# A block-diagonal inverse, a column-grouped projection and a segmented order in a gated mix of long convolution and local attention

## The chip, the cores and the metric

The kernel runs on one core of a Trainium2 chip. The metric is the time of one execution on the device, in microseconds. Three executions of the kernel before the change took 247.66, 249.07 and 249.46 us, so the median is 249.07. The profile comes from one more execution, which took 247.85 us; its instructions span 246.1 us.

Names used below: PE is the tensor engine (PEld its weight loads), DVE the vector engine, ACT the scalar engine, POOL the GpSimd engine, SP the engine that issues most of the DMAs.

## What is computed

With S = 2048 tokens, D = 640 channels and bf16 inputs:

```python
x = A_q
g = sigmoid((x * gate_w).sum(-1, keepdims=True))
# a: long convolution
k_shift = causal 4-tap filter of A_k with A_shift_k (per channel)
kv = k_shift * A_v
y  = irfft(rfft(pad(kv)) * rfft(pad(A_ssm_k)))[:S] + kv * A_ssm_D
a  = A_q * y
# b: 32 heads of 20, each token sees 8 keys at distance 0, 2, ..., 14
q, k, v = split(x @ B_wqkv)
b = softmax(local_scores(q, k) * 20**-0.5) @ v @ B_wo
out = g * a + (1 - g) * b
```

## The kernel before, in words

The long convolution is done as a transform of length 4096 in factors 32 x 64 x 2, with matmuls on PE. Channels are laid out as four groups of 160 on the four blocks of 32 partitions, with 32 positions of the first factor in each block. The channels are treated in two halves, P = 0 and P = 1.

- `xpose`, `vproj`, `qkproj` (L575) transpose x and project it. `fragger` (L614) moves pieces of projected q and k by DMAs from POOL into sets of four heads. `score_gen` (L636) makes scores, ACT takes their exponentials (L643), `pv_gen` (L664) multiplies them by v, and DVE normalises (L676: a product with the f32 reciprocal, repeated over the 20 channels of a head).
- `gate` (L542) computes the gate's logits with 20 matmuls of 128 rows by 32 columns, 512 wide, in the four column groups of PE; four DMAs on SP spread the result over `g_nat`, and DVE makes g and 1 - g of it.
- `conv` and `conv_v` make kv on DVE (L481, L488, L492).
- `h_stream` and `u_stream` transform the filter and kv: `s1_unit` (L697), then `s2_unit` (L713), each with a cast out of PSUM by ACT or DVE (L284, L286). `swaps` (L805, L807) exchange halves of the filter's spectrum between partitions through SP's DMA queue. `products` (L751) multiplies spectra on DVE.
- `inverse1` (L820) does the first half of the inverse transform, 10 units of 16 matmuls for each P, and casts the result into the tile UC.
- `op_tr` (L838) transposes the attention output into the tile oT; `outproj` (L854) projects it by wo in 16 tiles of 128 tokens: ten matmuls each, 512 and 128 columns wide, for five blocks of 128 channels. Each is scaled by 1 - g (`omg`) on its way to the tile bl (L858 on ACT, L860 on DVE). Tiles 4 to 15 come first, then 0 to 3.
- `load_q` (L873) loads q a second time, into the tile SX behind the filter's spectrum: token tiles 4 to 15 when the second transform stages are done, and 0 to 3 after the inverse's first half of P = 0, because they lie on what it reads.
- `final` does the rest for six groups of up to three token tiles. First the second half of the inverse (L893): for every token tile 32 matmuls of 32 rows by 32 columns, 160 wide, 512 in all, into two PSUM slots a group. Then six ACT activations of 128x320 with the scale g (L901), a product with q on DVE (L906), the sum with bl (L908), and four DMAs on SP (L911).

The order is not written out by hand. Every stage is a generator that yields requests (`Req`): the engines that may do it, an estimated cost, the events it depends on, and PSUM slots taken and given back (there are four, `Plan(4)`). `Plan.run` repeatedly picks the request with the smallest `start + 120 ns * priority` and emits its instructions. The instructions of each engine then run in that order, with semaphores for the real dependences. The priorities are one number for each stage (`PRI`); for casts that ACT or DVE may do, `lean` is added to ACT's estimated end. `paced` loads wait until the modelled DMA pipe is within `BG` ns of running dry. A request without work is given to "G" (POOL) or "S" (SP) at a cost of 1 ns.

The numbers of the planner are estimates of its author and are not measurements of this run. Its model of PE counts instructions (`mm`, a matmul and its weight load are two) and allows one page of `PAGE = 256` every `FETCH = 3600` ns.

Of the kernel before, what the change touches and what calls it, by code (L numbers as in the profile page):

```python
# [10 lines left out]
BF = mybir.dt.bfloat16  # L11
# [37 lines left out]
BG = 1266.0  # L49
# [6 lines left out]
def fft_consts():  # L56
# [24 lines left out]
    T = np.tile(T.reshape(32, 64 * 2 * 32), (4, 1))  # L81
# [49 lines left out]
class Req:  # L131


    def __init__(self, engs, cost=0.0, deps=(), take=0, give=(), n=0, move=0.0, pri=None, mode=None, bg=None, mm=0, lean=0.0):
        self.engs, self.cost, self.deps, self.take, self.give, self.n, self.move = engs, cost, deps, take, give, n, move
        self.pri, self.mode, self.bg, self.mm, self.lean = pri, mode, bg, mm, lean
# [4 lines left out]
LEAN_QK = -248.0  # L141
LEAN_V = 87.0
LEAN_H = -137.0
PRI = dict(loads=0, fragger=0, xpose=-9.2, score_gen=-8.6, pv_gen=-5.7, conv=-1.6, conv_v=-24.1, bulk=0, conv_end=0, qkproj=-4.2, vproj=-4.8,
           gate=-0.8, load_G=0, h_slot=0, p2_slot=10.2, u_slot=0, swaps=0, load_T=0, op_tr=4.7, outproj=37.5, load_q=0, products=6.3, final=-18.6,
           h_stream=(-3.7, -4.9), u_stream=(0.9, 2.5), inverse1=(33.7, 30.7))
# [4 lines left out]
class Plan:  # L151


    def __init__(self, nslots):
        self.at = dict(P=0.0, A=0.0, D=0.0, G=0.0, S=0.0, Q=0.0)
# [6 lines left out]
        self.lane = {"S": lane, "Q": lane, "G": []}  # L162
# [4 lines left out]
    def add(self, gen, pri):  # L167
        self.streams.append([pri, gen, next(gen)])
# [6 lines left out]
    def start(self, r, e):  # L175
# [3 lines left out]
        for d in r.deps:  # L179
            if d.t is None:  # L180
                return INF
            t = max(t, d.t + LAT.get((d.eng, e), 60.0))
# [9 lines left out]
    def best(self, r):  # L192
        found = []
        for e in r.engs:
            s = self.start(r, e)
            found.append((s + self.cost(r, e) + (r.lean if e == "A" else 0.0), s, e))
        end, s, e = min(found)
        return s + self.cost(r, e) if s < INF else INF, s, e

    def run(self):  # L200
        while self.streams:
            pick = None
            for k, (pri, gen, r) in enumerate(self.streams):
                end, st, e = self.best(r)
                if st == INF:
                    continue
                p = pri if r.pri is None else r.pri
# [5 lines left out]
            pri, gen, r = self.streams[k]  # L213
# [16 lines left out]
            self.at[e] = end  # L230
# [19 lines left out]
            try:  # L250
                self.streams[k][2] = gen.send(g)
            except StopIteration:
                del self.streams[k]
# [3 lines left out]
def kernel(  # L257
# [45 lines left out]
    g_nat = p0.tile([128, 16], F32, name="g_nat")  # L303
    omg = p0.tile([128, 16], F32, name="omg")
# [62 lines left out]
    def loads():  # L367
# [9 lines left out]
        for c in (1, 0):  # L377
            for q in range(4):
                yield from load(f"k{q}{c}", kin[32 * q:32 * q + 32, 3 + 32 * c:35 + 32 * c, :],
                                raw(k2, 32 * c * D + QC * q, [[64 * D, 32], [D, 32], [1, QC]]), 2000.0)  # L380
        for c in range(2):
            for q in range(4):
                yield from paced(f"v{q}{c}", vin[32 * q:32 * q + 32, c], raw(v2, QC * q + 80 * c, [[64 * D, 32], [D, 64], [1, 80]]), 2100.0)
        yield Req("S", 1.0, [ev("xtr")])
        h_lin = p0.tile([128, 80, 2, 64], BF, name="h_lin", tag="HL")
        st["h_lin"] = h_lin
        for P in range(2):
            for q in range(4):
                for c in range(2):
                    yield from paced(f"h{P}{q}{c}", h_lin[32 * q:32 * q + 32, PL * P:PL * P + PL, c, :],  # L390
                                     raw(A_ssm_k, (160 * q + 80 * c + PL * P) * S, [[64, 32], [S, PL], [1, 64]]), 1200.0)
# [12 lines left out]
    def load_G():  # L404
        yield Req("S", 1.0, [ev("conv"), ev("grow"), ev("vproj")])
# [9 lines left out]
    def load_T():  # L415
        yield Req("S", 1.0, [ev("p2")])
# [3 lines left out]
        yield Req("S", 1.0, [ev("hw1")])  # L420
        T = st["p2"].tile([128, 64, 2, 32], BF, name="T")
        st["T"] = T
        yield from load("T", st["T"][:], cf["T"].ap().rearrange("p (a r b) -> p a r b", a=64, r=2), 2700.0)
# [6 lines left out]
    def heads():  # L430
# [14 lines left out]
        for q in range(4):  # L445
            nc.gpsimd.dma_start(Dz[32 * q:32 * q + 1, :], raw(A_ssm_D, 160 * q, [[0, 1], [1, 160]]))
        for e in range(2):
            masks(e)
            if e == 0:
                for q in range(4):  # L450
                    nc.gpsimd.memset(kin[32 * q:32 * q + 1, 0:3, :], 0.0)
                    nc.gpsimd.dma_start(wraw[32 * q:32 * q + 32].rearrange("p c j -> p (c j)"), raw(A_shift_k, 4 * QC * q, [[0, 32], [1, 4 * QC]]))
# [499 lines left out]
```

## Time and profile before

| | us |
|---|---|
| three executions | 247.66, 249.07, 249.46 |
| profiled execution, on the device | 247.85 |
| its span of instructions | 246.1 |
| PE busy | 215.8 (88%) |
| DVE busy | 185.8 (76%) |
| ACT busy | 168.6 (69%) |
| POOL busy | 68.8 (28%) |
| PE in the chain that ended last | 49% of the span |
| mean granted PE clock | 0.9 |

The mean durations of a group overlap when instructions are pipelined; start-to-start distances in the timeline are the cost of one among many. The chain of waits follows back from the last instruction to what released it; "issue" in it is time in which an engine waited for nothing that the profile shows. Some matmul records can be missing from a trace.

Stages in time: x is transposed and projected from 10 us on; the first scores come at 44 us, the last exponentials at 138; the two transforms run from 115 to 183; projection tiles and the first half of the inverse fill 183 to 221; `final` runs from there to 241.5.

### The profile page before, as it was taken

What the parts mean: (1) busy time and instruction counts of PE and PEld (TensorE: products, weight loads), DVE (VectorE), ACT (ScalarE), POOL (GpSimd) and SP (SyncE); (2) the same over time, 40 slices, a digit from 0 to 9 for tenths busy, and PEclk for the clock granted to TensorE, in tenths of its full rate; (3) what the DMA queues carried; (4) which work ended last, traced back from release to release, by engine and by line L of the source; (5) the groups of instructions that cost most, each with busy time, mean ns of one, the idle gap of its engine ahead of it and who ended that gap; (6) DMA issues with size and microseconds to landing.
All of it is one profiled execution on the core that took longest, in us unless ns stands there. A gap on an engine that the chain in (4) does not pass through costs nothing.

```text
span 246.1 us, 8342 instructions
## 1 busy us (share of the span) xinstructions
PE 215.8 (88%) x3654; PEld 167.2 (68%) x3654; DVE 185.8 (76%) x220; ACT 168.6 (69%) x222; POOL 68.8 (28%) x147
## 2 busy tenths in 40 slices
PE   6799999899796999999999999896979999984590
PEld 2699887776464667565766788785867799983350
DVE  1424499999879999978788899995899993134942
ACT  2143543774478785789889799988375589768871
POOL 6699699106719144619000000000000000000000
PEclk9999999999999799995555599999799999999568
DMA  6999965898994959698910000699939910400754
GB/s 230 305 348 192 177 81 137 148 158 142 180 146 95 150 96 138 122 164 245 257 67 4 3 4 3 151 221 212 218 61 204 268 20 3 109 0 5 179 147 107
DMA packets 59580, 33.83 MB, mean 137 GB/s; under 512 B 49212, under 2 KB 56008, under 8 KB 58904
## 3 DMA queue, kind: packets, MB, share of 16 engines
q1 hardware_dynamic: 55192, 27.08, 55.0%
q0 software_dynamic: 3792, 5.81, 10.5%
q8 instruction: 28, 0.46, 0.9%
q10 hardware_dynamic: 560, 0.42, 0.5%
q14 instruction: 8, 0.07, 0.1%
HBM read 20.01 MB, written 2.62 MB: 92 GB/s over the span
## 4 chain that ended last, share of the span: by engine, by line
PE 49%; DMA 13%; POOL 13%; issue 9%; ACT 9%; DVE 4%; SPq 1%; ACTq 0%; POOLq 0%; DVEq 0%
PE op L854 10%; PE pj L575 9%; PE i L820 7%; PE O L664 6%; DMA Hw<-SX 5%; PE sc L636 5%; ACT ETall L643 4%; PE s L713 4%; DMA kb<-stg 3%; POOL qb L614 3%; DMA mm<-ca_mm 3%; DMA KX<-in_A_k_dram 3%; PE psv L528 2%; POOL kb L427 2%; POOL qb L428 2%
## 5 line engine op out<-in xcount | busy, mean ns | idle before, releaser
L643 ACT ACTIVATE ETall<-sc 121x912 bf16<-121x912 f32 (+1 forms) x80 | 63.4, 855 | 12.5 <-PE sc L636 11.6
L575 PE MATMUL pj<-xT,Wqk 128*128 128x342 bf16 (+1 forms) x300 | 49.0, 314 | 1.0 <-ACT ETall L643 0.6
L575 PEld LDWEIGHTS <-Wqk 128*128 128x128 bf16 x300 | 28.4, 98 | 15.8 <-issue 1.4
L481 DVE TENSOR_TENSOR KX<-KX 128x1760 bf16<-128x1760 bf16 (+1 forms) x24 | 27.6, 1161 | 4.3 <-issue 4.0
L614 POOL DMA_DIRECT2D qb<-stg x36 | 18.1, 505 | 36.8 <-PE sc L636 14.6
L528 PE MATMUL psv<-KX,xT 128*121 128x320 bf16 x180 | 27.3, 300 | 1.0 <-DVE xT L286 1.0
L636 PE MATMUL sc<-qb,kb 31*128 31x114 bf16 x576 | 23.4, 241 | 5.4 <-ACT ETall L643 2.0
L284 ACT CAST UC<-s 128x960 bf16<-128x960 f32 (+2 forms) x25 | 22.3, 971 | 7.9 <-PE s L713 6.7
L854 PE MATMUL op<-wo,oT 128*128 128x512 bf16 (+1 forms) x160 | 25.7, 322 | 0.0
L528 PEld LDWEIGHTS <-xT 128*121 128x121 bf16 x180 | 23.4, 134 | 2.2 <-issue 1.2
L713 PEld LDWEIGHTS <-SX 64*128 64x128 bf16 x512 | 19.5, 96 | 7.8 <-issue 7.0
L636 PEld LDWEIGHTS <-kb 31*128 31x128 bf16 x576 | 13.7, 104 | 15.1 <-issue 9.3
L284 ACT CAST stg<-pj 128x684 bf16<-128x684 f32 (+1 forms) x17 | 12.5, 746 | 14.9 <-PE pj L575 9.2
L284 ACT CAST VW<-psv 121x640 bf16<-121x640 f32 x15 | 10.4, 696 | 17.8 <-PE psv L528 17.8
L854 PEld LDWEIGHTS <-oT 128*128 128x128 bf16 x160 | 17.1, 150 | 7.4 <-issue 2.3
L286 DVE CAST UC<-s 128x1024 bf16<-128x1024 f32 (+1 forms) x17 | 19.5, 1195 | 0.0
L488 DVE TENSOR_TENSOR KX<-KX 128x1760 bf16<-128x1760 bf16 (+1 forms) x18 | 18.8, 1042 | 0.3
L614 POOL DMA_DIRECT2D kb<-stg x36 | 17.9, 505 | 3.4 <-ACT stg L284 2.9
L858 ACT ACTIVATE bl<-op,omg 128x640 bf16<-128x640 f32 x16 | 12.7, 794 | 8.6 <-PE op L854 8.6
L820 PE MATMUL i<-F,Hw 128*128 128x128 bf16 x160 | 18.3, 219 | 0.0
L286 DVE COPY xT<-tx 128x1280 bf16<-128x1280 bf16 x8 | 6.5, 824 | 15.6 <-PE tx L467 15.6
L664 PEld LDWEIGHTS <-ETall 121*128 121x128 bf16 x576 | 16.5, 100 | 2.5 <-issue 1.7
(73 smaller groups left out, 376.4 us busy)
## 6 DMA issues: line engine op xcount, KB each, us to landing
xn<-in_A_q_dram SPq DMA_DIRECT2D x8, 320.0 KB, 8.0
KX<-in_A_k_dram SPq DMA_DIRECT2D x8, 320.0 KB, 11.8
vin<-in_A_v_dram SPq DMA_DIRECT2D x8, 320.0 KB, 7.1
h_lin<-in_A_ssm_k_dram SPq DMA_DIRECT2D x16, 160.0 KB, 4.9
Hw<-SX SPq DMA_DIRECT2D x4, 640.0 KB, 7.8
Hw<-Hs SPq DMA_DIRECT2D x4, 640.0 KB, 11.9
out_dram<-SX SPq DMA_DIRECT2D x20, 120.0 KB, 2.2
kb<-stg POOLq DMA_DIRECT2D x28, 85.1 KB, 3.6
```

The lines of the kernel that those rows point to most:

```text
L284: nc.scalar.copy(dst, src)
L286: nc.vector.tensor_copy(dst, src)
L481: eng.tensor_tensor(d, kin[:, n + 3 - j:n + 3 - j + m, :], w.to_broadcast([128, m, QC]), ALU.mult)
L528: nc.tensor.matmul(ps[0:BK, n0 // 320, 0:320], lhsT=xT[:, dt, s0:s0 + BK], rhs=Wv[:, dt, n0:n1], start=(dt == 0), stop=(dt == NDT - 1))
L575: nc.tensor.matmul(ps[:, i, 0:n], lhsT=Wqk[:, dt, w, 128 * ft:128 * ft + 128], rhs=xT[:, dt, s0:s0 + n], start=(dt == 0), stop=(dt == NDT ...
L614: nc.gpsimd.dma_start(dst[r0:r0 + rows, 0:wd], stg[fa - f0:fb - f0, 0:wd])
L636: nc.tensor.matmul(sc[:, hh, BQ * bb:BQ * bb + BQ], lhsT=kb[r:r + DH + NF, BK * b:BK * b + 128], rhs=qb[r:r + DH + NF, BQ * b:BQ * b + BQ] ...
L643: nc.scalar.activation(ETall[0:BK, e, :, 0:BQ * nb], sc[0:BK, :, 0:BQ * nb], ACT.Exp, scale=SCALE)
L664: nc.tensor.matmul(O[:, (b - b0) // 6, c0:c0 + 21], lhsT=ETall[0:BK, e, hh, BQ * bb:BQ * bb + 128], rhs=VW[0:BK, b, 4 * t + h4, :], start= ...
L713: nc.tensor.matmul(ps[:, c, 160 * jj:160 * jj + 160], lhsT=st["G"][rows, j0 + jj, rr, :], rhs=Am[rows, rr].rearrange("p o (q j) l -> p j ( ...
L820: nc.tensor.matmul(d, lhsT=st[(key, P)][:, c, o + il // 4, :, il % 4], rhs=M[:, k, :], start=(k == 0), stop=(k == 1), skip_group_check=True)
L854: nc.tensor.matmul(op[:, n0:n1], lhsT=oT[:, ft].rearrange("p h m a -> p a (h m)")[:, t, :], rhs=wo[:, ft, n0:n1], start=(ft == 0), stop=(f ...
```

## The change

1. The constant T of the inverse's second half becomes block-diagonal: two groups of channels share a 64-row block, and one weight load of 64 x 64 serves both. To make neighbours fit, the groups are laid out in the order `CH = [0, 320, 160, 480]`. T grows from 1 MB to 2 MB, half of it zeros.
2. The token rows of the last stage are halved: a partition holds 320 channels of a token, 32 such half rows in place of 16 rows. `g_nat` and `omg` have 32 columns.
3. The projection runs as 40 matmuls of 128 rows by 32 columns, 320 wide, in four column groups, for each of 16 pairs of half rows.
4. g is multiplied into q on DVE ahead of time (`gate_q`), so ACT only copies out of PSUM, one instruction for up to three half rows with both PSUM halves. The output is written by SP and POOL.
5. The planner has an engine "Z" without time for requests without work, priorities and leans for every stage in segments (`step`, priorities, leans), `products` as one stream for each P, and `BG = 1808`.

```diff
+CH = [0, 320, 160, 480]
+BG = 1808.0
...
-    T = np.tile(T.reshape(32, 64 * 2 * 32), (4, 1))
+    Td = np.zeros((2, 2, 32, 64, 2, 2, 32))
+    for e in range(2):
+        Td[:, e, :, :, :, e, :] = T
+    T = Td.reshape(128, 64 * 2 * 64)
...
+    "outproj": (6, (62.7, 39.6, 1.6, 16.3, 242.3, 242.3), (-531, -531, -531, -531, -531, -531)),
+    "gate_q": (3, (13.5, 8.6), (0, 0)),
+    "final": (15, (13.8, 10.8, 14.5), (0, 0, 0)),
+    "products0": (11, (2.2, -2.3), (0, 0)),
+    "products1": (11, (-1, -12.3), (0, 0)),
...
+    "inverse10": (11, (36.3, 233.3), (501, 776)),
+    "inverse11": (11, (8.9, -10.3), (-438, -880)),
+}
...
+    def pri(self, k):
+        (step, pri, _), n, r = self.streams[k][0], self.streams[k][3], self.streams[k][2]
+        return pri[min(n // step, len(pri) - 1)] if r.pri is None else r.pri
...
-        T = st["p2"].tile([128, 64, 2, 32], BF, name="T")
+        T = st["p2"].tile([128, 64, 2, 64], BF, name="T")
...
-        for t in (*range(4, 16), *range(4)):
-            g = yield Req("P", 5 * (215.0 + 56.0), [ev(f"oT{ft}") for ft in range(NDT)], take=1, mode="f", mm=10)
...
+        for t in (*range(8, 32, 2), *range(0, 8, 2)):
+            g = yield Req("P", 40 * 33.3 + 60.0, [ev(f"oT{ft}") for ft in range(NDT)], take=1, mode="g", mm=40)
+            op = psum(g, "op")
+            for tt in range(2):
+                h, a = divmod(t + tt, 16)
+                for ft in range(NDT):
+                    for e in range(2):
+                        for w in range(2):
+                            c = 64 * e + 32 * w
+                            nc.tensor.matmul(op[c:c + 32, tt, 0:320], lhsT=oT[:, ft, h, 32 * e:32 * e + 32, a], rhs=wo[:, ft, 320 * w:320 * w + 320],
+                                             start=(ft == 0), stop=(ft == NDT - 1), tile_position=(0, c), skip_group_check=True)
+            r = yield Req("AD", dict(A=1080.0, D=820.0), [g.done], give=g.banks)
             if r.eng == "A":
+                for tt in range(2):
+                    nc.scalar.activation(bl[:, t + tt, :], op[:, tt, 0:320], ACT.Copy, scale=omg[:, t + tt:t + tt + 1])
             else:
+                nc.vector.tensor_tensor(bl[:, t:t + 2, :], op[:, :, 0:320], omg[:, t:t + 2].unsqueeze(2).to_broadcast([128, 2, 320]), ALU.mult)
...
+    def gate_q():
+        for a, b in ((8, 14), (14, 20), (20, 26), (26, 32), (0, 4), (4, 8)):
+            r = yield Req("D", 150.0 + 0.53 * 320 * (b - a), [ev("ql0" if a < 8 else "ql8"), ev("gate")])
+            reg = st["qg"][:, a:b, :]
+            nc.vector.tensor_tensor(reg, reg, g_nat[:, a:b].unsqueeze(2).to_broadcast([128, b - a, 320]), ALU.mult)
+            mark(f"qg{a}", r)
...
+        yb4 = st["SX"][:, 0:3840].rearrange("p (k t n) -> p k t n", k=4, t=3)
+        ybfree = [Ev(0.0)] * 4
+        for n, (t0, m) in enumerate([(t, 3) for t in range(8, 32, 3)] + [(0, 3), (3, 3), (6, 2)]):
+            g = yield Req("P", m * 8 * 28.0 + 30.0, [ev("Cm0"), ev("Cm1"), ev("T")], take=1, mode="u", mm=m * 8)
...
+                    for e in range(2):
+                        n2 = 2 * (t0 + tt) + e
+                        for qp in range(2):
+                            rows = slice(64 * qp, 64 * qp + 64)
+                            nc.tensor.matmul(ps[64 * e:64 * e + 64, qp, 160 * tt:160 * tt + 160], lhsT=T[rows, n2, r, :],
...
+            r = yield Req("A", 160.0 + 0.84 * 320 * m, [g.done, ybfree[n % 4], ev("i10")], give=g.banks)
+            nc.scalar.copy(yb[:, 0:m, :].rearrange("p t (q c) -> p q t c", q=2), ps[:, :, 0:160 * m].rearrange("p q (t c) -> p q t c", t=m))
...
+            if n < 8 and n % 2 == 0:
+                continue
+            a = t0 - 3 if n < 8 else t0
+            reg = st["qg"][:, a:t0 + m, :]
+            for e in range(2):
+                for w in range(2):
+                    (nc.gpsimd if w else nc.sync).dma_start(raw(outf, (e + 2 * a) * D + 320 * w, [[64 * D, 32], [2 * D, t0 + m - a], [1, 320]]),
+                                                            reg[64 * e + 32 * w:64 * e + 32 * w + 32])
```

## The prediction, on record before the changed kernel ran

> **What bounds the kernel now.** I read the windows by stage first, to learn which engine is full where, then the chain of waits and the tensor engine's timeline from 183 us on, then single groups for prices.
>
> ```profile
> 44.50:183.50 139.00, 126.12 (x2346) 95.00 (x2344) 124.28 (x144) 107.50 (x133) 32.11 (x83) 0.86 0.70 130
> 183.50:199.00 15.50, 15.50 (x127) 11.80 (x127) 15.50 (x29) 9.62 (x13) 0.00 (x0) 1.00 0.88 197
> 205.30:220.90 15.60, 14.51 (x230) 13.72 (x228) 3.67 (x3) 12.38 (x14) 0.00 (x0) 1.00 0.19 44
> 220.90:241.50 20.60, 13.14 (x542) 8.35 (x541) 12.48 (x12) 16.10 (x35) 0.00 (x0) 0.75 0.39 102
> 241.50:246.10 4.60, 0.00 (x0) 0.00 (x0) 0.00 (x0) 0.00 (x0) 0.00 (x0) 0.83 0.48 128
> ```
>
> Behind each stretch stand its length, the busy time of PE, PEld, DVE, ACT and POOL, the clock, the DMA share and GB/s. Up to 220.9 the tensor engine is close to full, so time there is its work. Call the end of the last cast out of the inverse's first half F: it is at 220.87. Behind F nothing is full: ACT 16.1 of 20.6 us, PE 13.1, DVE 12.5. From 241.5 on only output DMAs run.
>
> ```profile
> 210.88 8.95 PE i L820 x160
> 219.82 0.02 issue
> 219.84 1.02 ACT UC L284
> ...
> 222.58 1.78 issue
> ...
> 226.06 2.61 ACT yb L901 x6
> ...
> 233.21 5.09 PE op L854 x20
> 238.29 0.29 PE i L893 x32
> 238.58 1.56 PE op L854 x10
> ```
>
> The chain behind F alternates between PE without instructions ("issue"), ACT's evictions (L901), and three projection tiles (L854), of which two ran at half clock: 5.09 us for 20 matmuls, against 14.16 us for 100 before F, which is 1.41 us a tile.
>
> ```profile
> 220.91 1.67 PE L893 MATMUL i<-UC,T 32*32 32x160 bf16 x168 [1.10 <-ACT UC L284]
> 224.36 1.28 PE L893 MATMUL i<-UC,T 32*32 32x160 bf16 x120 [1.78 <-issue]
> ...
> 228.09 1.19 PE L893 MATMUL i<-UC,T 32*32 32x160 bf16 x90 [0.28 <-issue]
> ...
> 232.37 0.84 PE L893 MATMUL i<-UC,T 32*32 32x160 bf16 x56 [1.70 <-issue]
> ```
>
> The small matmuls run in bursts at about 10 ns each and then stop; PE is released at 224.36, 228.09 and 232.37, with 128 matmuls listed from each release to the next (the rows not shown counted). That is 29 to 33 ns for a matmul with its weight load, a supply rate and not arithmetic.
>
> **Part by part: the last stage.** *Inverse matmuls.* 512 of 32x32 become 256 of 64x64. At 29 ns the supply costs 7.4 us in place of 14.8, and in the tail it no longer leads.
>
> *Evictions.* ACT had 32 activations of 128x320. Six back to back take 2.61 us, 0.43 each, 13.8 us. Now there are ten copies of 128x960 and one of 128x640. The cast of 128x960 from PSUM has mean 968 ns, and four back to back take 3.66, 0.92 each: 9.9 us in all.
>
> *VectorE.* L906 and L908 moved 1920 elements in 1.16 us; now the unit is 960 elements, which L751 takes in 0.57 back to back. Eleven units cost 20 x 0.57 + 2 x 0.41 = 12.2 us, as before (12.5).
>
> *The gate on VectorE* is new: q times g over 32 half rows, 10,240 elements, with g in f32 repeated along the row. Two rows bound it:
>
> ```profile
> L676 DVE TENSOR_TENSOR oS<-O,rd 114x480 bf16<-114x480 f32 x24 | 15.0, 654 | 0.6
> L906 DVE TENSOR_TENSOR SX<-yb,SX 128x1920 bf16<-128x1920 bf16 x5 | 5.8, 1159 | 6.3 <-ACT yb L901 6.2
> ```
>
> L906 (bf16 only) gives (1159 - 484)/1280 = 0.53 ns an element, the figure in the new request's own cost. L676 multiplies by an f32 reciprocal repeated along the row, as the gate product does, though its other operand is in PSUM: some 1.05 ns with 150 fixed. I take 1.05, as the nearest row in operands: 10.8 us plus 6 x 0.1. The Trainium skill, "VectorE: DVE Perf Modes", section "What auto-detection actually checks", speaks against this part: two elements a cycle need every tensor to be 16-bit with step 1, which g is not; by the other price the forecast would be 1.4 us lower. The 24 rows loaded first (8.3 us) lie in 205 to 220, where DVE idles 11.9 us; were that cover gone, the tail would start up to 3.6 us late (8.3 less the 4.7 that the plan counts). The other 8 rows cannot: their q overwrites what the last inverse matmuls read, so they load after F and cost the tail 2 x 1.4 = 2.8 us.
>
> *Projection.* 16 tiles of 10 matmuls become 16 of 40, each 128 rows by 32 columns and 320 wide. The same form is the gate matmul, 20 of 512 columns in 1.19 us on the chain, 59.5 ns each, so its four column groups do overlap. Scaled by 320/512: 37 ns, 1.49 us a tile. Bounds: 28 ns (48 matmuls of L664, 21 columns, in 1.35 us), 1.12 us; and 59.5 ns with no gain from fewer columns, 2.38 us. I take 1.49, as the only row with this tiling. ACT's part is two activations, 0.86 for 0.79; DVE's 820 is not used in before, and the lean of -531 ns toward ACT makes it rare. The last four tiles (t = 0 to 6) get priority 242.3, 29 us late, so they stand behind F; before it was three. Before F: 12 x 0.08 - 1.41 = -0.45 us.
>
> *The tail after F.* First unit 24 matmuls, then ACT, so DVE starts near F + 1.65; 12.2 + 2.8 us later it ends: F + 16.65. ACT: 9.9 + 4 x 0.86 = 13.3. PE: 7.4 + 6.0 = 13.4. So DVE is what is late next, and the tail is 16.65 in place of 20.6: -3.95. If the clock halves as in before, four tiles take 4 x 2.98 and start when the banks free, near F + 5.5: F + 17.4, then eviction and sums, about F + 19; that is 2.3 back.
>
> *Output.* 28 transfers on two queues in place of 24 on SP. In the last group SP issues 2 rather than 4 (0.43 each, -0.86); POOL's issue is 0.505 and its smallest qb and kb transfers land in 2.5 to 4.8 against SP's 1.6, +0.6 or more. I take zero. POOL has no work after 120 us, so nothing queues behind these.
>
> *Loads.* T is 1 MB larger: 5.3 us at the 197 GB/s of 183.5 to 199. It moves the q loads behind it on SP by as much, into a stretch (199 to 205.3) with a DMA share of 0.00, and they are used after 205; without that cover 5.3. The gate's transfers stay four, 2 KB becoming 4 KB. Column order (CH), the wider g_nat and the zero-cost requests change no work: nothing, at most 0.2.
>
> **The order.** Everything ahead is planned anew: priorities in segments, pacing (BG) 0.5 us earlier, other choices of evicting engine. No row prices an order. From 44.5 to 183.5 PE idles 12.9 us and the clock is 0.86; in 110 to 141, where the exps keep ACT at 27.2 of 31, it is 0.52. Bounds: an order that recovers 8 us of idle time and clock, or one that loses 5, about the longest waits listed (5.6 for POOL on a score, 5.3 for ACT on the v projection). I take -2.
>
> **Sum.** From the profiled execution, 247.85 (span 246.1 and 1.75 around it): -0.45 - 3.95 + 0 - 2 = 241.45. The median of three is 249.07, 1.2 above that execution; I add half: 242.
>
> **Rivals.**
> *Slower: weight loads bound the column-grouped projection.* It issues 640 loads in place of 160, all from oT with a stride of 16 elements, and L854's loads are already slow (150 ns against 98 for Wqk). At 59.5 ns a matmul: 12 x (2.38 - 1.41) - 1.41 = +10.2 before F, a tail of 9.5 + 7.4 = 16.9, the order -2: 253. It decides from 51 ns on, where 12 tiles cost 7.4 us more. Against it: the gate's row, at 512 columns. The Trainium skill, "TensorE: Matmul & The Clock Gate", Part 3 ("Packing small matmuls"), "The mechanism", says that weight loads overlap matmuls in flight only where the row group differs, and here all four groups share every row; by that rule the pair would not go below its load, and the gate's 59.5 ns against loads of 96 ns speaks against it. Chance 0.10.
> *The order gives the gain back* (+5 where I took -2, by one long wait on a score set or a swap): 249. The planner's costs are estimates, and it counts the gate product at half of mine. Chance 0.17.
> *The order gains much* (-8): 236. For it: 12.9 us of idle PE and a half clock of 30 us; against: DVE and ACT are full there too, 124 and 108 of 139. Chance 0.22.
> That the change doesn't do what it says I leave out: the counts of matmuls follow from the code.
>
> **How the numbers follow.** Forecast 0.47, its own range 239 to 246; other mishaps, such as the q loads or the half clock together, 0.04 on the slow side. The range takes in the order's gain and most of the case that gives it back: 234.5 to 250.5. A measurement here tells about 1% from no change (three runs span 0.7%). Faster than 246.6: the forecast, the large gain, a third of the give-back: 0.74. Within 1%: 0.12. Slower: the weight loads, the mishaps: 0.14.
>
> **What would show it.** L893's successor: 256 matmuls, no "issue" above 1 us behind F. ACT's copies at 0.92; the gate products at 2.0 us for 1920 elements, not 1.1. The projection's 40 matmuls in 1.5 us at full clock. DVE the fullest engine from F on, F at 218 to 220, and F to the last DVE end 16 to 17 us. It is wrong if F moves by more than 8 us, or if the last sum waits for a projection tile.

## The result, and the profile after

The changed kernel took 282.15 us, the median of four runs (280.46 to 284.95), beside 249.26 for the kernel before on the same chip: a ratio of 1.132 [1.121, 1.143] (in brackets, here and below, the 95% interval). Executions of one kernel fall into a faster and a slower group; ratios compare the faster ones alone, and a time without a ratio beside it is the median of all. The profiled execution took 280.46 us with a span of 278.3. Lines of the changed kernel stand some 33 below those of before (the products, L751 before, are L775; the second half of the inverse is L925).

| us from the span's start | before | after |
|---|---|---|
| last exponentials end | 137.8 | 144.4 |
| swap transfers issued | from 154.7 and from 166.3 | all eight from 180.3 |
| first product of spectra | 170.7 | 208.4 |
| F, the end of inverse1's last cast | 220.9 | 247.2 |
| last sum ends | 241.5 | 267.5 |
| end of the span | 246.1 | 278.3 |

So 26 us were lost ahead of F, the tail from F to the last sum is about as long as before (20.3 for 20.6), and 6.2 more went behind the last sum. These are the windows by stage; behind each stretch stand its length, then the busy time of PE, PEld, DVE, ACT and POOL, the clock, the DMA share and GB/s.

```profile
181.30:192.60 11.30, 10.27 (x290) 9.63 (x294) 0.00 (x0) 8.50 (x16) 0.00 (x0) 1.00 1.01 221
192.60:208.30 15.70, 3.00 (x89) 2.70 (x78) 0.00 (x0) 2.83 (x6) 0.00 (x0) 0.70 1.02 226
247.00:267.50 20.50, 13.82 (x416) 11.58 (x416) 16.25 (x25) 13.45 (x19) 6.33 (x12) 0.83 0.58 135
267.50:278.30 10.80, 0.00 (x0) 0.00 (x0) 0.04 (x1) 0.00 (x0) 1.47 (x3) 0.65 0.17 48
```

For 27 us, from 181.3 to 208.3, DVE does nothing, and in the last 15.7 of them PE and ACT hardly anything. The DMA engines are full. The waits (engine, line, what it waited for, total us, times, longest us) say for what:

```profile
ACT UC L317 <- PE i L843: 29.0, 4, 26.0
DVE Hs L775 <- DMA Hw<-Hs: 28.3, 1, 28.3
PEld L843 <- DVE Hs L775: 25.0, 1, 25.0
...
DVE KX L521 <- DMA g_nat<-KX: 6.0, 1, 6.0
...
DVE SX L908 <- DMA SX<-in_A_q_dram: 3.7, 1, 3.7
```

All three engines wait for one thing, the swap of the second half of the filter's spectrum. SP's queue (start, time, line) shows that this swap isn't slow but late:

```profile
180.33 0.55 SPq L828 DMA_DIRECT2D Hw<-SX  x1
...
186.50 2.41 SPq L828 DMA_DIRECT2D Hw<-Hs  x1
...
192.64 1.37 SPq L830 DMA_DIRECT2D Hw<-Hs  x1
194.32 1.50 SPq L389 DMA_DIRECT2D T<-cf_T  x1
195.92 51.57 SPq L901 DMA_DIRECT2D SX<-in_A_q_dram  x8
```

The first swap is issued at 180.33, when the filter's last cast is done; before, that cast ended at 154.7. The swaps of both halves then go out together, and the products begin with P = 1, whose swap lands last.

**Why the plan let this happen.** The new engine "Z" has no clock in the planner (`if e != "Z": self.at[e] = end`). Before, "wait for the filter's spectrum" was a request to SP, and moved SP's time in the plan to that event; the swap transfers behind it started there. Now the wait is a request to Z, and the transfers, without a dependence of their own (`Req("S", 650.0, move=3050.0)`), are planned as if they could go at once. Followed through, the change's plan has the swaps at 117 to 122 of its own microseconds and their data ready only at 177. T and q hang on waits of the same form. The instructions are still correct, since semaphores carry the real dependences; but the order that every engine executes was chosen for data that are not there.

The chain at the tail (start, length, what):

```profile
247.04 3.72 DMA SX<-in_A_q_dram
...
252.29 1.49 DVE SX L908
253.78 0.58 DVE SX L934
254.38 0.66 DVE SX L937
```

DVE waits 3.7 us for q and then multiplies eight half rows by the gate before it begins the first group of `final`. That group uses other half rows and could have gone first, but DVE runs its queue in the planned order.

### The profile page after: what moved, and what is told of

It is laid out like the page before. It is cut to its first block, busy times and chain, and to the rows that moved or that the text cites. A ratio compares the mean times of both kernels' runs of the same rounds, so it can differ in the third digit from the quotient of the medians.

```text
span 278.3 us, 8846 instructions
## 1 busy us (share of the span) xinstructions
PE 217.4 (78%) x3878; PEld 176.1 (63%) x3878; DVE 193.7 (70%) x233; ACT 167.4 (60%) x220; POOL 77.8 (28%) x161
## 4 chain that ended last, share of the span: by engine, by line
PE 57%; DVE 15%; DMA 9%; ACT 7%; issue 4%; SPq 2%; POOL 1%; POOLq 0%; DVEq 0%; ACTq 0%
PE pj L609 14%; PE psv L561 9%; PE i L843 7%; PE O L698 6%; DMA Hw<-Hs 6%; ACT ETall L677 5%; PE sc L670 5%; PE op L881 4%; PE s L747 4%; DVE Hw L775 2%; PE s L731 2%; PE tx L500 2%; DVE SX L937 2%; DVE SX L934 2%; DVE Hs L775 2%
## 5 line engine op out<-in xcount | busy, mean ns | idle before, releaser
L944 POOL DMA_DIRECT2D out_dram<-SX x14 | 7.8, 562 | 136.5 <-DVE SX L934 133.5
L317 ACT CAST UC<-i 128x1024 bf16<-128x1024 f32 x15 | 14.3, 1032 | 30.6 <-PE i L843 29.0
L843 PE MATMUL i<-F,Hs 128*128 128x128 bf16 x80 | 11.8, 250 | 24.8 <-DVE Hs L775 24.8
L317 ACT CAST UC<-s 128x960 bf16<-128x960 f32 (+2 forms) x31 | 28.0, 992 | 1.9 <-PE s L747 1.1
L775 DVE TENSOR_TENSOR Hs<-UC,Hs 128x960 bf16<-128x960 bf16 (+1 forms) x11 | 7.0, 637 | 28.3 <-DMA Hw<-Hs 28.3
L514 DVE TENSOR_TENSOR KX<-KX 128x1760 bf16<-128x1760 bf16 (+1 forms) x24 | 25.2, 1061 | 1.7 <-DMA KX<-in_A_k_dram 1.1
L881 PE MATMUL op<-wo,oT 128*32 128x320 bf16 x640 | 25.2, 316 | 1.3 <-issue 1.0
L843 PEld LDWEIGHTS <-Hs 128*128 128x128 bf16 x80 | 10.0, 126 | 25.0 <-DVE Hs L775 25.0
L881 PEld LDWEIGHTS <-oT 128*32 128x32 bf16 x640 | 22.8, 142 | 2.9 <-issue 1.7
L521 DVE TENSOR_TENSOR KX<-KX 128x1760 bf16<-128x1760 bf16 (+1 forms) x18 | 18.8, 1044 | 6.5 <-DMA g_nat<-KX 6.0
L317 ACT CAST VW<-psv 121x640 bf16<-121x640 f32 x17 | 11.9, 702 | 17.0 <-PE psv L561 17.0
L670 PEld LDWEIGHTS <-kb 31*128 31x128 bf16 x576 | 13.8, 103 | 12.0 <-issue 10.0
L747 PEld LDWEIGHTS <-SX 64*128 64x128 bf16 x512 | 19.2, 95 | 3.3 <-issue 2.7
```

Of the source, the lines that this page charges most:

```text
L317: nc.scalar.copy(dst, src)
L514: eng.tensor_tensor(d, kin[:, n + 3 - j:n + 3 - j + m, :], w.to_broadcast([128, m, QC]), ALU.mult)
L521: eng.tensor_tensor(ta if j else dst, ta, tb, ALU.add)
L670: nc.tensor.matmul(sc[:, hh, BQ * bb:BQ * bb + BQ], lhsT=kb[r:r + DH + NF, BK * b:BK * b + 128], rhs=qb[r:r + DH + NF, BQ * b:BQ * b + BQ] ...
L747: nc.tensor.matmul(ps[:, c, 160 * jj:160 * jj + 160], lhsT=st["G"][rows, j0 + jj, rr, :], rhs=Am[rows, rr].rearrange("p o (q j) l -> p j ( ...
L775: nc.vector.tensor_tensor(X, U, X, ALU.mult)
```

## The experiments

Ratios are against the kernel before, run beside each. "Told" below means that the waits are visible to the planner, as in the first edit.

**Told waits.**

```diff
-            yield Req("Z", 0.0, outs("h", P) + ...)
+            z = yield Req("Z", 0.0, outs("h", P) + ...)
...
-                r = yield Req("S", 650.0, move=3050.0)
+                r = yield Req("S", 650.0, [z.done], move=3050.0)
```

and the same for the loads of T and q.

> The changed kernel, where the requests for the swap, T and q loads are told the time of the wait in front of them; tables of priorities as in the change. Theory 1 (the planner no longer sees that the swaps of the filter's spectrum wait for its transform, and so plans the products of P = 1 first although P = 0 is swapped first): products of P = 0 start when the first swap lands, near 194 instead of 208.4, F moves from 247 to about 235, time 268 (264 to 272). The spectrum itself is still late (it ends near 180), so it does not come back to 249. Rival (the tables alone put the spectrum late, and who is first of the products is worth nothing): 279 to 282, products at 208.

Measured: 269.71 us, 1.074 [1.063, 1.085]; the products start at 197.8 and F is at 238.7, near what was expected. The edit changes no work and gives back 12 us (14 by the ratios): that much is the hidden wait.

**The order of before, waits hidden and told.** Priorities, leans and `BG` as before, first without the told waits:

> The changed kernel with the priorities, leans and BG of before, one number for each stage. Theory 1 (the order costs the 32 us): the spectrum ends near 155, F at 220 to 227, time 250 to 260, of which some 6 are the wait at the very end behind POOL's output transfers. Rival (the new last stage is slow in itself): 270 or more with the spectrum early.

Measured: 277.57, 1.105 [1.088, 1.123], a miss by 18 us and what the rival said; the run after it decides between the two. The swaps are early again (158.3 and 169.9), but T (2 MB) is issued ahead of q, and the blind plan has put the gate products ahead of DVE's copies of oT:

```profile
203.57 2.16 DVE L891 TENSOR_TENSOR SX<-SX,g_nat 128x1920 bf16<-128x1920 bf16 x1 [19.21 <-DMA SX<-in_A_q_dram]
205.65 1.22 DVE L302 COPY oT<-tr 128x2048 bf16<-128x2048 bf16 x1
```

In this timeline (start, length, what; in brackets the idle time before it) DVE stands 19.21 us for q, and the projection waits for the oT copy behind. The same with the told waits:

> The changed kernel with the priorities of before, and the S requests told the time of the wait in front of them. Theory (in a2 the plan put the gate products on DVE before the transposes, because it took q as loaded at 164 when the load started at 184): DVE no longer waits 19 us for q, so F near 229 and 255 to 261, with 6 us at the end behind POOL. Rival (the new stage is slow in itself whatever the plan knows): 270 or more.

Measured: 259.12, 1.035 [1.023, 1.048], as expected. Told waits are worth 18 us under the order of before and 12 under the change's. Under told waits the order of before is 10 us better than the change's tables; which of priorities, leans and `BG` does it wasn't separated.

**The old last stage.** First under the change's planner and tables:

> The changed kernel with the last stage of before (32x32 inverse matmuls, projection of 512 and 128 columns, g in the evictions, outputs on SP) under the new planner and tables. Theory 1: products start at 208 as in the change, F near 247, time 270 to 276, so the loss is there without the new stage. Rival (the new stage is slow): 245 to 255.

Measured: 275.41, 1.097 [1.080, 1.113]. DVE waits 27.2 us for the swap there too: the loss ahead of F isn't the new stage's. Then the old last stage with told waits and the order of before. This kernel also has the old column order (`CH = [0, 160, 320, 480]`) and the `g_nat` of 16 columns, as a3_old_stage has, though the expectation says otherwise; only the new planner and the form of the waits are left of the change:

> The last stage of before and the order of before (flat priorities, leans, BG), with the change's column order, wide g_nat and requests without time, the waits of the swaps, of T and of q told to the planner. Theory: the requests without time do harm only where a wait is hidden from the planner, and the column order and the wide g_nat cost little, so this is the kernel before again: 250 us, 248 to 253. Then what a6_old_order_waits has above it (some 9 us) is the new last stage by itself, under an order that wasn't made for it. Rival: column order, wide g_nat or requests without time cost as much by themselves: 255 to 259, as a6_old_order_waits.

Measured: 248.27, 0.999 [0.994, 1.004]: the kernel before again. What a6_old_order_waits has above it, 9 to 11 us, belongs to the new last stage with the column order and the wide `g_nat`. No run takes these two apart from the stage, but the traces say where the time goes. Up to the first swap a6_old_order_waits is not behind (issued at 153.2 and, in a10_old_stage_told, 154.7), so the new layout of the loads costs nothing there. In the profiled executions (257.59 and 244.41 us) F is at 229.5 in place of 215.7, the tail is 15.3 in place of 22.3, and 11.0 us in place of 4.6 follow the last sum. Part of the first two is a shift: a6_old_order_waits has all sixteen projection tiles ahead of F, where the other has four behind it.

**Single suspects, in the changed kernel.** All outputs issued by SP:

```diff
-                    (nc.gpsimd if w else nc.sync).dma_start(
+                    nc.sync.dma_start(
```

> The changed kernel with all 28 output transfers issued by SP. Theory: POOL's last drain (9.2 us in the trace of the change, after its last transfer is issued at 268.4) is what ends the span, so without transfers on POOL at the end the span is 5 to 6.5 us shorter: 274 to 275.5 on the device where the change takes 280.5. Rival (the end waits for the data, not for POOL): within 1.5 us of the change, or longer by the 0.4 us that each further issue on SP takes.

Measured: 280.06, a miss for the 274 to 275.5 expected. The last sum ends at 268.6 and the span at 276.6, 8.0 later in place of 10.8. SP needs until 273.9 to issue 28 transfers, so most of the gain goes into that queue. The gate's rows read by eight DMAs of one partition each, in place of four that cover conv's tile in between:

```diff
-            nc.sync.dma_start(g_nat[32 * gg:32 * gg + 32, :], raw(src, 64 * (gg // 2) * pt, [[32 * pt, 2], [32, 16], [1, 32]]))
+            for i in range(2):
+                nc.sync.dma_start(g_nat[32 * gg + 16 * i:32 * gg + 16 * i + 16, :],
+                                  raw(src, (64 * (gg // 2) + 32 * i) * pt, [[pt, 1], [32, 16], [1, 32]]))
```

> The changed kernel, with the gate's rows read by eight transfers of one partition each rather than four of two partitions; the plan's order is the same. Theory: the convolution on DVE waits for the gate's transfers (6.0 us at 65 to 71 in the change) only because a transfer that spans two partitions is taken to cover the tile KX between them; with one partition each the wait is gone, DVE and PE are 5 to 6 us ahead from 72 us on and the swaps start near 175: 275 (274 to 277). Rival (the 6 us are absorbed before the spectrum is ready, by the scores or the queue of POOL): 279 to 282.

Measured: 281.35, 1.124 [1.116, 1.133]. The 6.0 us wait of DVE is gone and the swaps still go out at 181.6: the rival was right, the wait cost nothing that set the end. A bf16 copy of g in the gate products (`g_bf` for `g_nat`):

> The changed kernel with g copied to bf16 for the gate product on VectorE; the operand is still repeated along the row (step 0). The Trainium skill, VectorE: DVE Perf Modes, What auto-detection actually checks, asks for 16-bit tensors with step 1 or -1. If the f32 type alone cost the second element per cycle: 1920 elements in 1.15 us. If step 0 does as well: 2.07 us as in the change. The time of the kernel hardly moves (within 3 us of the change).

Measured: 281.06 in one run, and these are the groups of that line in the changed kernel and, in the second fence, in this one (ns: least, median, most):

```profile
L908 DVE TENSOR_TENSOR SX<-SX,g_nat x6: 1485/2157/2159, 232.8 to 252.3; 128x1920 bf16<-128x1920 bf16 x4, 128x1280 bf16<-128x1280 bf16 x2
```

```profile
L910 DVE TENSOR_TENSOR SX<-SX,g_bf x6: 1484/2138/2142, 233.3 to 252.9; 128x1920 bf16<-128x1920 bf16 x4, 128x1280 bf16<-128x1280 bf16 x2
```

The type isn't what holds it at 1.1 ns an element, where two bf16 operands without a repeat took 1.16 us for 1920 (0.6 ns). The Trainium skill, "VectorE: DVE Perf Modes", section "What auto-detection actually checks", asks for 16-bit tensors with step 1; g repeated along the row has step 0, and the 2.14 us agree.

**Mending the new stage, with told waits and the order of before.**

```diff
-            nc.vector.tensor_tensor(reg, reg, g_nat[:, a:b].unsqueeze(2).to_broadcast([128, b - a, 320]), ALU.mult)
+            for t in range(a, b):
+                reg = st["qg"][:, t, :]
+                nc.vector.tensor_scalar(reg, reg, g_nat[:, t:t + 1], None, ALU.mult)
...
-                    (nc.gpsimd if w else nc.sync).dma_start(
+                    ((nc.scalar if n == 10 else nc.sync if n > 7 else nc.gpsimd) if w else nc.sync).dma_start(
```

with the gate rows as above.

> As a6, and mended: gate rows as in a5, the gate product as 32 tensor_scalar instructions of 320 bf16 elements with g as a scalar for each partition, and POOL issues no output after the first eight groups (SP and, in the last group, ACT). Theory: the gate product takes 0.2 us a half row (6.4 in place of 11.3), the end is 4.6 to 5.5 us after the last sum, F near 225: 244 to 251, no slower than before by more than 1%. Rival (the new stage gains nothing over the old in this order): 252 to 258.

Measured: 253.56, 1.014 [1.009, 1.019], above the 244 to 251 that were expected and in the rival's range. The 24 gate products take 5.20 us in place of 8.4. The tail from F (228.5) to the last sum is 15.3, with all projection tiles and gate products ahead of F. What is left lies ahead of F: DVE stands 3.40 us for q and then does the gate products with spectra still to multiply behind them. Moved to GpSimd, which is idle (`nc.gpsimd.tensor_scalar`, requested from "G"):

> a7_old_order_mended with the 32 products of q and gate (tensor_scalar, 128x320 each) on GpSimd in place of VectorE. Theory: what a7_old_order_mended still loses against the kernel before lies ahead of the end of inverse1's casts, because VectorE runs 24 gate products there (5.2 us) and stands 3.4 us for q's load ahead of inverse1's evictions; GpSimd has nothing to do from 124 us to 233 us. Without them VectorE reaches the end of inverse1 some 5 us earlier: 248.5 us, 246 to 250.5, and no wait of VectorE for q's load ahead of inverse1's evictions. Rival: GpSimd's products slow VectorE's own, or take so long that the sums wait for them: 252 to 258.

Measured: 258.18, 1.034 [1.029, 1.040]. F came 4 us earlier, but part of that is again a shift: four projection tiles are behind it now. The tail is 20.1 us in place of 15.3, and 12.3 us in place of 6.8 follow the last sum, since a product takes 1.07 us on GpSimd and its outputs queue behind the last eight. The rival was right.

**A new order.** Priorities, leans and `BG` chosen anew by the planner's own end, in two versions; both also take GpSimd out of the outputs behind the fourth group, and have the plan hold the first gate products 3 us longer:

> a7_old_order_mended (new last stage, told waits, the gate product in 32 tensor_scalar on VectorE) with priorities, leans and BG chosen anew so that the planner's own end comes out early: 233.3 of its us, where a7_old_order_mended has 240.6; the gate products stand behind all products of spectra, and the last three output groups issue on SP and ACT. Theory: once the planner knows the waits its end can be trusted to some 3 us (a7_old_order_mended: 240.6 planned, last sum at 243.9), so the last sum comes at 236 to 238 and the time at 244, 241.5 to 247.5: faster than the kernel before. Rival: an order tuned on the planner's estimates gains nothing on the chip, as the change's own tables did: 250 to 256.

> As a11_new_order with another set of priorities, leans and BG (planned end 234.0). Theory: 244.5, 242 to 248, within 1% of a11_new_order, since both plans end within 0.7 of each other. Rival: the two differ by more than 2%, so that the planned end says little at this grain.

Measured: 258.99 (four executions at 253.50, 258.82, 259.15 and 259.64, too far apart for a ratio) and 259.31, 1.041 [1.034, 1.047], where the plans ended 7 us earlier than for a7_old_order_mended. Both miss the 244 that were expected, and the rival of the first was right: an order tuned on the planner's estimates gained nothing on the chip. The projection is one place where its costs don't hold. The tensor engine's timeline of a6_old_order_waits (start, length, line and operation, number; in brackets the idle time before):

```profile
186.74 6.25 PE L864 MATMUL op<-wo,oT 128*32 128x320 bf16 x128 [3.77 <-issue]
...
195.95 9.87 PE L864 MATMUL op<-wo,oT 128*32 128x320 bf16 x284 [2.96 <-issue]
```

PE has nothing to execute for 3.77 us, then executes 128 projection matmuls, 256 instructions with their weight loads, and again has nothing for 2.96. From 179.6 to 205.8 its 504 projection matmuls took 52 ns each. The gaps are not all of it: the 128 matmuls behind the first one ran at a granted clock of 0.73, 49 ns each, and those behind the second at 1.00, 35 ns each. In a12_new_order_b such gaps ahead of the projection and of the transforms' second stage come to 10.3 us. A reading of it: instructions come in pieces of 256, by the DMA engines that are moving swaps, T and q at that time. The times of single DMA packets in the trace bear it out: the queue for instructions brought a packet of 16 KB by 185.18 and the next by 194.65, and PE went on at 186.74 and 195.95. So traffic was taken away. T loaded as soon as its memory is free, at 124 us, in place of behind the swaps:

```diff
-        z = yield Req("Z", 0.0, [ev("hw1")])
+        z = yield Req("Z", 0.0, [ev("p2")])
         T = st["p2"].tile([128, 64, 2, 64], BF, name="T")
```

> a7_old_order_mended with the load of T (2 MB) issued as soon as its memory is free, some 60 us earlier, in place of behind the swaps. Theory: what the new last stage still loses lies between 180 and 205 us, where the column-grouped projection (640 matmuls in place of 160, each with its weight load) runs while swaps, q and T are moved: PE runs out of instructions after every 128 matmuls, because its instructions come by the same DMA engines; 473 projection matmuls took 22.3 us there (47 ns each) against 35 ns where nothing is moved. With T's 2 MB gone from this stretch the matmuls behind 195 us run at 35 to 40 ns: 1 to 3 us, 251.5 us (250 to 253). Rival: the gaps are PE waiting for its weights or banks: no change, 253.5.

Measured: 251.28, 1.005 [0.998, 1.012], the time that was expected, but not by the way expected: the 504 matmuls of the projection's stretch took 22.1 us, beside 22.3 in a7_old_order_mended, with gaps of 2.9 beside 2.8, and 1.005 isn't told apart from 1.014. T had been behind q in the queue, too late to matter much, and the stretch began 1.2 us earlier.

The plan's wait of q's first load moved to the end of inverse1's matmuls of P = 0 (`ev("i10")`):

> As a13_T_early, and q's first load (1.9 MB) too leaves the stretch: it waits for the end of inverse1's matmuls of P = 0. Theory: behind the swaps nothing is moved while the projection runs: its matmuls at 36 to 40 ns (4 us), no wait of VectorE for q ahead of inverse1's evictions (3.4 us in a7_old_order_mended), 247 us (244 to 250). Rival: q then comes late for the gate products and the tail gives it back: 252 to 256.

Measured: 246.18, 0.983 [0.970, 0.997]: faster than the kernel before, but not for the reason given. Only the plan held q's load back; SP issued it at 182.5, as in a13_T_early (179.0). What changed is that DVE has the gate products behind all products of spectra, and waits for no q.

The same with a second `load("T", ...)` behind `ev("hw1")`:

> As a14_T_early_q_late, with T loaded a second time behind the swaps (the same bytes into the same place, for nobody before the last stage): only traffic is added. Theory: gaps come back in the projection, its matmuls at 42 to 50 ns, and the time is 2 to 4 us above a14_T_early_q_late. Rival: traffic doesn't matter to PE, and the time is that of a14_T_early_q_late within 1 us.

Measured: 250.67, 1.011 [1.005, 1.016], 4.5 us above the same kernel without the second load of T, more than the 2 to 4 expected; the plans of the two give every engine the same order but for that load. The gaps of PE ahead of projection matmuls come to 6.5 us, beside 2.5 in a14_T_early_q_late, and the 124 matmuls behind the longer gap took 58 ns each at a granted clock of 0.61. Traffic alone costs the projection time, in gaps and in the clock behind them.

In a13_T_early, the place of the gate products named to the planner, and GpSimd out of the outputs behind the fourth group:

```diff
-            r = yield Req("D", 200.0 * (b - a), [ev("ql0" if a < 8 else "ql8"), ev("gate")])
+            r = yield Req("D", 200.0 * (b - a), [ev("ql0" if a < 8 else "ql8"), ev("gate"), ev("Cm1" if a < 8 else "mult1")])
...
-                    ((nc.scalar if n == 10 else nc.sync if n > 7 else nc.gpsimd) if w else nc.sync).dma_start(
+                    ((nc.gpsimd if n <= 3 else nc.scalar if n >= 8 else nc.sync) if w else nc.sync).dma_start(
```

> a13_T_early with the 24 gate products ordered behind the last product of spectra (plan: 208.6 to 213.4) and the other eight behind inverse1's casts, and the last output groups issued by SP and ACT. The first load of q stays where it is (SP issues it at about 180 us in a13_T_early and a14_T_early_q_late alike, since only the plan, not the queue, held it back there). Theory: VectorE has nothing to do between the products (end 208) and the last casts of inverse1; with the gate products there, the last casts are shared by two engines again: 244.5, 242 to 247, against 246.2 in a14_T_early_q_late. Rival: the order is worth nothing more, the tensor engine sets the end of inverse1: 246 to 249.

Measured: 247.61, 0.987 [0.977, 0.998], in the rival's range and not told apart from a14_T_early_q_late. Then, in this kernel, q's first load was truly moved:

```diff
-                r = yield Req("S", 650.0, [z.done], ...)
-                nc.sync.dma_start(qg[32 * g:32 * g + 32, a:b], ...)
+                r = yield Req("S" if n else "A", 650.0, [z.done], ...)
+                (nc.sync if n else nc.scalar).dma_start(qg[32 * g:32 * g + 32, a:b], ...)
```

with z behind the ninth projection tile.

> As a16_gate_between, and q's first load is issued by ScalarE behind the ninth projection tile, so that it truly leaves the stretch with the projection (1.9 MB). Theory: the projection's matmuls go from about 50 ns each to 36 to 42, and inverse1 (128 columns, 57 ns a matmul) needs fewer instructions a microsecond and bears the traffic: 242.5, 240 to 245. Rival: ScalarE's four issues and the later q cost as much: 245 to 249.

Measured: 243.70, 0.979 [0.970, 0.988], as expected and the fastest kernel of the study, though its interval overlaps those of a14_T_early_q_late and a16_gate_between. The tensor engine's timeline of it, and below it that of a15_traffic_back:

```profile
183.31 11.91 PE L866 MATMUL op<-wo,oT 128*32 128x320 bf16 x344 [0.17 <-DVE oT L302]
```

```profile
183.16 3.35 PE L868 MATMUL op<-wo,oT 128*32 128x320 bf16 x92 [0.61 <-DVE oT L302]
188.09 4.58 PE L868 MATMUL op<-wo,oT 128*32 128x320 bf16 x128 [1.58 <-issue]
197.58 7.18 PE L868 MATMUL op<-wo,oT 128*32 128x320 bf16 x124 [4.91 <-issue]
```

And the windows of the same stretch, of a17_q_after_projection and then of a15_traffic_back:

```profile
182.00:190.00 8.00, 7.83 (x212) 7.17 (x216) 7.97 (x14) 3.95 (x9) 0.00 (x0) 0.94 0.01 2
190.00:198.00 8.00, 8.00 (x218) 7.47 (x211) 8.00 (x16) 4.56 (x10) 0.00 (x0) 1.00 0.15 39
```

```profile
182.00:190.00 8.00, 5.81 (x164) 5.22 (x160) 8.00 (x14) 2.84 (x6) 0.00 (x0) 1.00 0.99 282
190.00:198.00 8.00, 3.09 (x88) 2.72 (x84) 8.00 (x15) 1.89 (x4) 0.00 (x0) 0.90 1.14 173
```

Without traffic 344 matmuls run without a gap at 35 ns each; with 282 and 173 GB/s beside them the same 16 us hold 252 matmuls of all kinds in place of 430. The control is the old projection with T moved in the same way:

> a10_old_stage_told with T (here 1 MB) loaded as soon as its memory is free. Theory: the old projection has 160 matmuls of up to 512 columns, so PE isn't short of instructions beside the traffic and has no gaps to lose: the time of a10_old_stage_told, 248.3, 247 to 250. Rival: taking T out of the stretch behind the swaps helps the old last stage as much as the new one (2.3 us): 246.

Measured: 247.46, 0.994 [0.988, 0.999], beside 0.999 [0.994, 1.004] with T late: at most a small gain. The old projection, with a quarter of the instructions, shows no gap of PE there. Whether the old stage would gain from a later q wasn't tried, so it isn't shown that the new stage is the better one where both have their loads well placed.

## Why the prediction was wrong, point by point

The forecast was 242 us, and the kernel took 282.15. Its own sign of being wrong, F moving by more than 8 us, came true: F moved by 26. Taken apart by a1_plan_waits, a6_old_order_waits and a10_old_stage_told (1.132, 1.074, 1.035, 0.999), the hidden waits cost 12 to 14 us, the tables of the order some 10, and the last stage 9 to 11, where the forecast had at most 0.2, -2 and -4.4.

**The step that failed first** is a clause: "Column order (CH), the wider g_nat and the zero-cost requests change no work: nothing, at most 0.2." They do change no work, and of the column order and g_nat the traces show no cost. But the requests without time were where the planner learned of a wait. Priced by the runs, that clause is worth 12 us (told waits in the changed kernel) to 18 (under the order of before). The code needed to follow it was there: a request to Z leaves no trace in `at`, and the next request to SP names no dependence.

**The order**, "I take -2", bounds -8 to +5: with told waits the change's tables cost 10 us against those of before, outside the bounds. They were taken from idle time in the trace of before, which can say what an order may recover. It can't say what a new one may lose.

**The rival that came nearest in size** was the projection, and its mechanism was wrong. Weight loads don't bound it: four tiles took 5.62 us in the changed kernel, 1.41 each for the 1.49 forecast, 35 ns a matmul, with loads of 142 ns in the mean. The rule quoted there from the Trainium skill, "TensorE: Matmul & The Clock Gate", Part 3, doesn't hold for this tiling by these runs: loads and matmuls of four column groups overlap. What does cost is the number of instructions beside traffic: 52 ns a matmul in a6_old_order_waits, some 8.6 us over its 504 matmuls (26.2 less 504 x 35 ns), 6.7 of them in gaps and 1.8 in the slower matmuls behind the first gap. With the four tiles that moved ahead of F (160 x 35 ns, 5.6 us) that is about the 13.8 us by which F is later than in a10_old_stage_told; the shorter tail gives 7.0 back, and the output takes 6.4. I had read the supply of instructions (29 to 33 ns for a matmul with its load) in the tail, where the DMA share is 0.39, and used it only there; the projection runs where the share is near 1.

**The tail**, -3.95: next to nothing was gained in the changed kernel (20.3 us for 20.6, where 16.65 was forecast). The forecast had 1.65 us to the first unit, 2.8 for eight gate products and 12.2 for the eleven units. The plan put the gate products, and with them the wait for q, ahead of the units, so DVE began 3.7 us behind F. The gate products took 2.9, and the units 13.85: a unit's product and the sum that needs it take 1.27 us, not 2 x 0.57, the price of independent products. In a1_plan_waits, with the same work behind F in a better order, the tail is 18.4. The 15.3 of a7_old_order_mended are no test of the forecast, since they hold no gate product and no projection tile.

**The output**, "I take zero", bounds -0.86 to +0.6: it cost 6.2. The bounds counted issues and landings. In the runs, the span ends about 9 us after POOL's last transfer is issued; with POOL out of the last groups it ends 3.5 us after the last sum (a17_q_after_projection).

**Right in size:** the gate product at 1.05 ns an element (8.36 us for the 24 half rows, 8.3 forecast, 2.89 for the eight, 2.8), ACT's copies (0.89 to 0.99 for 0.92), the matmuls of the inverse's second half (most groups of 24 in 0.61 us, 26 ns each, for 29; one took 1.01 us). **Loads:** the forecast said 5.3 us if T's cover for q is gone; in a2_old_order DVE waited 19.2, for T's load, q's own and the early place of the gate products together.

## What to carry to other kernels

Where a planner orders the work, a request that costs nothing can still carry a time: before removing it, list every request that started later because of it, and give those the dependence by name. Count instructions as a resource beside bytes: a stage that is cut into four times as many matmuls wants a stretch without bulk transfers, or, as here, loses to its own instruction supply. And an end that comes earlier in a plan is worth only as much as the costs that the plan holds; of two plans 7 us better, one was some 6 us worse on the chip (259.31 beside 253.56) and the other no better.

## What the runs showed of the hardware

PE's gaps at the column-grouped projection came in steps of 128 matmuls with their loads, 256 instructions, and beside bulk transfers: from 1.0 us in the changed kernel, where the swap is waited for anyway, to 7.3 in a1_plan_waits; none in a17_q_after_projection. The list of DMA queues of the changed kernel (packets, MB, share of 16 engines) has one for instructions:

```profile
q8 instruction: 30, 0.49, 0.8%
```

That is 16 KB a packet, and 30 packets for PE's 7756 instructions (3878 matmuls and as many loads), 259 a packet. All 16 gaps of over 1.2 us ahead of projection matmuls in which PE waited for no engine (in 12 of the traces) ended 1.2 to 1.8 us after such a packet had come in. So PE waits for these packets. That they are late because they stand behind the bulk ones is the reading that fits; the runs show the dependence on traffic.

GpSimd's last output transfer ties the end: it was issued by 268.97, 246.45, 241.83 and 247.78 us in the changed kernel, a6_old_order_waits, a7_old_order_mended and a9_gate_on_pool, and the spans ended 9.3, 9.4, 8.9 and 8.8 us later. SP's last issue was at 247.38 in a7_old_order_mended, 3.3 us before the end, beside 2.7 in a4_out_on_sp, where GpSimd issues none; so only the other three tell the two causes well apart.

GpSimd and VectorE hold each other up. In a9_gate_on_pool the products on GpSimd read:

```profile
L894 POOL TENSOR_SCALAR SX<-SX,g_nat x32: 1072/1074/13678, 193.4 to 242.1; 128x320 bf16<-128x320 bf16 x32
```

One of the 32 took 13.68 us in place of 1.07. It is the first, from 193.4 to 207.0, and VectorE's unbroken run of two-input products ended at 206.1. The Trainium skill, "SBUF — State Buffer", section "SBUF: two separate sides", has an exclusive lock on a shared pair of ports that a VectorE instruction with two SBUF inputs holds for its whole length; this row agrees, and shows that a run of such instructions without pauses keeps GpSimd out to its end. Later the exclusion is not complete: from 228.1 to 240.0 VectorE's eight pairs of product and sum take 1.47 us each in place of 1.27, and eight products on GpSimd beside them 1.49 in place of 1.07, where one after the other they would take 2.3.

A product with a scalar for each partition (TENSOR_SCALAR, 128x320 bf16) takes 0.22 us on VectorE, 24 in 5.20, where the product with g repeated along the row takes 0.35 (8.36 for 24).
